# Attention on one core: shape blocks on TensorE in the step that forms scores, transposes and multiplies by v

## The chip, the cores and the metric

The kernel runs on one core of a Trainium2 chip. The metric is the device time of one execution in microseconds, the median of several runs.

## The reference, cut to what matters

Causal attention with a learned decay, for 4 batches of 8 heads with 576 positions and head size 64, in float32; then two feed-forward blocks on the 2304 tokens of 512 numbers.

```python
scores = scale * np.matmul(q, k.transpose(0, 1, 3, 2))
cum = np.cumsum(np.maximum(s, 0.0), axis=-1)
bias = -(cum[:, :, :, None] - cum[:, :, None, :])
scores = np.where(causal, -1000000000.0, scores + np.minimum(bias, 0.0))
scores = scores - np.max(scores, axis=-1, keepdims=True)
attn = np.exp(scores)
attn = attn / (np.sum(attn, axis=-1, keepdims=True) + 1e-09)
x = np.matmul(attn, v)                 # then heads side by side: (2304, 512)
a = x @ w1
b = x @ w2
x = (a * b @ w3) @ w_out               # first block
h = x @ w_in                           # second: softmax, a norm, and w_out
```

## The kernel before

**Work of a head.** The queries of a head are cut into five row tiles (the table QT): four of 128 rows, which see 576, 448, 320 and 192 keys, and one of 64 rows, which sees 64 keys. `qk_part(h, part)` forms the scores of tile 0 in a large PSUM buffer (part 0, two products of 288 columns), of tiles 1 and 4 in a small one (part 1), of tiles 2 and 3 in another (part 2), and `softmax_tile` (lines 205 and 209) takes the row maximum on VectorE and the exponential on ScalarE. Heads 0 to 7 form scores by one float32 product each (line 183), later heads by two of a faster type (lines 191 and 192), whose operands `split_qk` prepares. `normalise(h)` divides the rows by their sums (lines 236 to 244).

`tr_part(h, part)` transposes the weights of head h through TensorE into PSUM, and `evict` copies them into the tile PT of that head, on ScalarE and VectorE in turn (lines 92 and 94). Parts 0, 1 and 2 hold four, four and two transpositions of 128 by 128 (line 276). Three kinds of 64-by-64 blocks remain: the one of tile 4 (line 280, in part 2, on rows 0 to 63, issued behind the eviction of part 2's 256 columns from the same PSUM bank), and the four lower halves of the diagonal blocks (line 284, part 3, on rows 64 to 127). A head has fifteen transpositions and seven evictions.

`av_parts(p)` multiplies the transposed weights of a pair of heads with v. It makes twelve products of two heads each (line 308); each float32 product stands in the trace as two passes, so a pair has 24 records. The first is a product of 64 columns on 64 rows, then come 512, 448, 320 and 192 columns on 128 rows, and the last, for the keys 512 to 575, has 64 columns on 64 rows. The result is evicted from a large PSUM buffer into xT, as a coarse and a fine half. v is loaded by `load_v` into a tile `vr` with two buffers.

**Fillers.** `ab_unit` computes half a block of a and b, twelve products of 288 columns for each (line 336), for batches whose attention is done. Each of its two functions goes into the list `fill`.

**Order.** The loop from line 511 writes one step after the other. A step forms the scores of head h, transposes head ph = h - 2 and, behind every second one, has the products with v of that pair. NF says how many units a step adds to `fill`; F(1) to F(4) issue a quarter of the list each, at four places: between the parts of the scores, behind the first part of the transpositions, behind the third, and at the end. Pairs from head 10 on have their products with v put off: they become one entry, third in the next step's `fill`. At a step's end stand the loads for v and for the head after next (q, k and the rows of the cumulated sums, all on SyncE's queue) and `split_qk`.

This is the order of the program text. The framework's scheduler gives it to the engines by priority in that order, but moves an instruction ahead of others that it believes to be waiting, so the order on an engine can differ. From step 11 on, PSUM holds one large buffer (for scores of tile 0 and the products with v) and six small ones (for all else).

After attention the memory of its tiles is given back, and the stage loads of w3 and the first w_out begin (line 416), beside the a and b units of the last batch; then come the second block's products.

The few lines that set the order of a step:

```python
        if h is not None:
            qk_part(h, 1)
            F(1)
            qk_part(h, 2)
        if ph is not None:
            tr_part(ph, 0)
        F(2)
```

Of the kernel before, what the change touches and what calls it, by code (L numbers as in the profile page):

```python
# [8 lines left out]
F32 = mybir.dt.float32  # L9
# [16 lines left out]
def tile_attention_moe(  # L26
# [15 lines left out]
    nc = tc.nc  # L42
    B, H, D, _, S = qkT.shape
# [17 lines left out]
    QOF = {4: QT[0][3], 3: QT[1][3], 2: QT[2][3], 1: QT[3][3], 0: QT[4][3]}  # L61
# [13 lines left out]
    ident = const.tile([128, 128], F32, name="ident")  # L75
# [8 lines left out]
    def smalltile(name):  # L84
        return PSP[1].tile([128, 512], F32, tag="B", name=name)

    def flat(ap):
        return ap.rearrange("p a b -> p (a b)")

    def hi(dst, src, eng=None):  # L90
        if eng is None:
            nc.scalar.activation(out=dst, in_=src, func=AF.Copy)  # L92
        else:
            eng.tensor_copy(out=dst, in_=src)

    def lo(dst, src, hi_, eng=nc.vector):
        eng.tensor_tensor(out=dst, in0=src, in1=hi_.bitcast(F32), op=ALU.subtract)  # L97
# [3 lines left out]
    at = attn_ctx.enter_context(tc.tile_pool(name="at", bufs=1, side="left"))  # L101
# [12 lines left out]
    PT = [at.tile([128, KO[5]], F32, name=f"PT{i}") for i in range(4)]  # L114
# [1 line left out]

    after = [None]
    raw_t = {}
    v_t = {}
    VB = 2  # L120
    XHE = None

    def load_head(h):
# [12 lines left out]

    def load_v(p):
        b, hp = divmod(p, NP)
        vr = at.tile([128, 5, 2, D], F32, tag="vr", bufs=VB, name="vr")
        v_t[p] = vr  # L140
        nc.sync.dma_start(
            out=vr[:, 0:4].rearrange("p c e d -> p (c e d)"), in_=vM[b, hp],
        )
        nc.sync.dma_start(out=vr[0:64, 4].rearrange("p e d -> p (e d)"), in_=vE[b, hp])
# [10 lines left out]
    def ENG(h):  # L155
        if h < 8:
            return dict(QB=None, KA=None, QA=V, QL=G, KL=V)
        return dict(QB=None, KA=None, QA=V, QL=G, KL=G)
# [3 lines left out]
    def split_qk(h):  # L162
        if h < NQ:
            return
        q2, k2 = raw_t.pop(h)
        QA = at.tile([128, S], F32R, tag="QA", bufs=2, name="QA")
        KA = at.tile([128, S], F32R, tag="KA", bufs=2, name="KA")
        qb, kb = QB[h % 2], KB[h % 2]
        e = ENG(h)
        hi(qb[64:128], q2[64:128], e["QB"])  # L170
        hi(KA, k2, e["KA"])
        hi(QA[0:64], q2[0:64], e["QA"])
        lo(QA[64:128], q2[64:128], qb[64:128], e["QL"])
        lo(kb[64:128], k2[64:128], KA[64:128], e["KL"])
        qk_t[h] = (QA, KA)
# [70 lines left out]
    def half_view(t, j):  # L246
        a = t[0:64, KO[j]:KO[j] + 64]
        return bass.AP(a.tensor, a.offset, [list(a.ap[0]), [S - 128 * j, 2], [1, 64]])

    def tr_part(h, part):  # L250
        pt = p_t[h]
        PT_ = PT[h % 4]
        ps = smalltile("tr")

        def evict(dst, src):
            cnt[0] += 1
            hi(dst(PT_), src, PCOPY[cnt[0] % len(PCOPY)])

        def blk(j, q0, q1):
            o = KO[j] - 128 * j  # L260
            return lambda t: t[:, o + q0:o + q1]

        ev = []
        if part == 0:
            full = [(0, i, (i - 1) * 128) for i in range(1, 5)]
            ev = [(0, 512, blk(0, 64, S))]
        elif part == 1:
            full = [(1, i, (i - 2) * 128) for i in range(2, 5)] + [(3, 4, 384)]
            ev = [(0, 384, blk(1, 192, S)), (384, 512, blk(3, 448, S))]
        elif part == 2:  # L270
            full = [(2, i, (i - 3) * 128) for i in range(3, 5)]
            ev = [(0, 256, blk(2, 320, S))]
        else:
            full = []
        for j, i, c in full:
            nc.tensor.transpose(ps[:, c:c + 128], pt[:, QOF[i] + 128 * j:QOF[i] + 128 * j + 128], ident)  # L276
        for c0, c1, d in ev:
            evict(d, ps[:, c0:c1])
        if part == 2:
            nc.tensor.transpose(ps[0:64, 256:320], pt[0:64, QOF[0]:QOF[0] + 64], ident[0:64, 0:64])  # L280
            evict(lambda t: t[0:64, 0:64], ps[0:64, 256:320])
        if part == 3:
            for i in range(1, 5):
                nc.tensor.transpose(
                    ps[0:64, 64 * i:64 * i + 64],
                    pt[64:128, QOF[i] + 128 * i:QOF[i] + 128 * i + 64],
                    ident[64:128, 64:128],
                )
            for j in (1, 3):
                src = ps[0:64, 64 * j:64 * j + 128].rearrange("p (a b) -> p a b", a=2)  # L290
                evict(lambda t: half_view(t, j), src)
            p_t.pop(h)
# [3 lines left out]

    def av_parts(p):

        vr = v_t.pop(p)
        b, hp = divmod(p, NP)  # L300
        XH, XL = xT[b % 2]
        st = {}

        def mm(j, c0, c1, **kw):
            rows = 64 if j == 4 or c1 == 64 else 128
            o = KO[j] - 128 * j
            for e in range(2):
                nc.tensor.matmul(  # L308
                    st["ps"][64 * e:64 * e + 64, 448 + c0:448 + c1], vr[0:rows, j, e],
                    PT[(2 * p + e) % 4][0:rows, o + c0:o + c1], **kw,  # L310
                )

        def part(j):
            if j == 0:
                st["ps"] = flat(bigtile("av"))
                mm(0, 0, 64, start=True, stop=True)
            mm(j, 128 * j if j else 64, S, start=j == 0, stop=j == 4)
            if j == 4:
                ps = st["ps"]
                hi(XH[:, hp], ps[:, 448:1024], XHE)  # L320
                lo(XL[:, hp], ps[:, 448:1024], XH[:, hp])

        return [lambda j=j: part(j) for j in range(5)]
# [163 lines left out]
    for st in STAT:  # L487
        nc.gpsimd.memset(st, 1.0)
    for t in PT:
        for j in range(1, 4):  # L490
            nc.gpsimd.memset(t[64:128, KO[j]:KO[j] + 64], 0.0)
    split_qk(0)
    if NQ < 1:
        load_head(1)
# [9 lines left out]
    steps += [(None, H - 2), (None, H - 1)]  # L504
    steps += [(h if h < NH else None, h - 2 if h >= H + 2 else None) for h in range(H, NH + 2)]
    NF = {10: 3, 11: 0, 12: 3, 13: 0, 14: 3, 15: 2, 16: 2, 17: 0, 18: 1, 19: 1, 20: 1, 21: 2, 22: 2, 23: 2, 24: 2, 25: 2, 26: 2, 27: 2, 28: 2, 29: 2, 30: 2, 31: 2, 32: 2, 33: 2, 34: 3, 35: 3}
    PD, AVO = 10, 2
    PUMP = {3: 1, 5: 1, 6: 1, 10: 2, 11: 1, 12: 2, 13: 1, 14: 3, 15: 2, 16: 1, 17: 1}
    fill = []
    late = []  # L510
    for st, (h, ph) in enumerate(steps):
        for _ in range(NF.get(st, 0)):
            fill.extend(ab_unit(*units.pop(0)))
        if late:
            parts = late.pop()
            fill.insert(min(AVO, len(fill)), lambda parts=parts: [fn() for fn in parts])
        left = len(fill)
        if st == 11:
            ps_ctx.close()
            PSP[:] = [  # L520
                ps_ctx.enter_context(tc.tile_pool(name="psE", bufs=1, space=PSUM)),
                ps_ctx.enter_context(tc.tile_pool(name="psF", bufs=6, space=PSUM)),
            ]

        def F(k):
            while fill and len(fill) > left * (4 - k) // 4:
                fill.pop(0)()

        if h is not None:
            if NQ <= h + 2 < NH:  # L530
                load_head(h + 2)
            qk_part(h, 0)
        if st > 1:
            pump(PUMP.get(st, 0))
        if h is not None:
            qk_part(h, 1)
            F(1)
            qk_part(h, 2)
        if ph is not None:
            tr_part(ph, 0)  # L540
        F(2)
        if h is not None:
            normalise(h)
        if ph is not None:
            tr_part(ph, 1)
            tr_part(ph, 2)
            F(3)
            tr_part(ph, 3)
        if h is not None:
            if h % 2 == 1:  # L550
                load_v(h // 2)
            if h + 1 < NH:
                split_qk(h + 1)
            if h < 2 and h + 2 < NQ:
                aug_rows(QB[h], KB[h])
            if h + 2 < NH:
                if h + 2 < NQ:
                    load_head(h + 2)
                load_aug(h + 2, cumf_scr[h + 2:h + 3] if h + 2 < NQ else cum_scr[h + 2])
        F(4)  # L560
        if ph is not None and ph % 2:
            parts = av_parts(ph // 2)
            if ph < PD or st == len(steps) - 1:
                for fn in parts:
                    fn()
            else:
                late.append(parts)
# [180 lines left out]
    for i in range(8):  # L748
        c, o = divmod(i, 2)
# [48 lines left out]
    for t in range(NT + 2):  # L798
        c, o = divmod(t, 2)
# [68 lines left out]
```

## Time and profile before

| what | us |
|---|---|
| median of 3 runs (lowest, highest) | 797.59 (797.01, 799.87) |
| profiled execution | 799.96 |
| its span, first to last instruction | 798.1 |
| TensorE busy (products) | 767.1 (96%) |
| VectorE busy | 474.7 (59%) |
| ScalarE busy | 396.2 (50%) |
| GpSimd busy | 154.2 (19%) |
| mean granted clock of TensorE | 0.985 of full |

The profile is that of one execution. TensorE's products (PE) are pipelined: a product's record lasts longer than the time until the next one starts, and its end is modelled. So two times can be read: the length of a record, and the distance of two starts. PEld are the weight loads, which overlap the products. DVE is VectorE, ACT ScalarE, POOL GpSimd and SP SyncE; L336 is line 336 of the kernel. A form like 128\*64 is rows by columns of the loaded weights; 64x64 f32 behind it is what is written.

### The profile page before, as it was taken

What the parts mean: (1) busy time and instruction counts of PE and PEld (TensorE: products, weight loads), DVE (VectorE), ACT (ScalarE), POOL (GpSimd) and SP (SyncE); (2) the same over time, 40 slices, a digit from 0 to 9 for tenths busy, and PEclk for the clock granted to TensorE, in tenths of its full rate; (3) what the DMA queues carried; (4) which work ended last, traced back from release to release, by engine and by line L of the source; (5) the groups of instructions that cost most, each with busy time, mean ns of one, the idle gap of its engine ahead of it and who ended that gap; (6) DMA issues with size and microseconds to landing.
All of it is one profiled execution on the core that took longest, in us unless ns stands there. A gap on an engine that the chain in (4) does not pass through costs nothing.

```text
span 798.1 us, 13047 instructions
## 1 busy us (share of the span) xinstructions
PE 767.1 (96%) x4864; PEld 655.5 (82%) x4864; DVE 474.7 (59%) x1162; ACT 396.2 (50%) x927; POOL 154.2 (19%) x155
## 2 busy tenths in 40 slices
PE   7988899999999999999989979899999999999997
PEld 5555888878988888898988868788888888888886
DVE  5897699866565555325977999744344243533231
ACT  4986697896666566322435435533323233332232
POOL 6031323242122121002323345300000000000000
PEclk9998999999999999999999989899999999999999
DMA  5542465333332320105759555012020200000001
GB/s 145 180 138 81 120 193 175 87 119 92 105 90 77 105 61 31 46 30 177 239 167 315 187 184 185 15 53 67 14 67 23 70 14 14 14 14 14 14 27 39
DMA packets 38038, 75.58 MB, mean 95 GB/s; under 512 B 6796, under 2 KB 18060, under 8 KB 37976
## 3 DMA queue, kind: packets, MB, share of 16 engines
q1 hardware_dynamic: 37976, 74.76, 30.2%
q8 instruction: 38, 0.62, 0.3%
q14 instruction: 24, 0.20, 0.1%
HBM read 60.36 MB, written 14.38 MB: 94 GB/s over the span
## 4 chain that ended last, share of the span: by engine, by line
PE 77%; DVE 9%; DMA 6%; POOL 3%; issue 2%; ACT 1%; SPq 1%; POOLq 0%; ACTq 0%; DVEq 0%
PE o L737 13%; PE b L336 12%; PE a L336 11%; PE h L688 11%; PE x L668 10%; PE av L308 6%; PE tr L276 4%; DMA stage<-in_w_dram 3%; PE sc L191 2%; PE sc L192 2%; DVE stage L379 2%; PE tr L726 2%; PE sc L183 2%; DVE stage L378 2%; DVE stage L382 1%
## 5 line engine op out<-in xcount | busy, mean ns | idle before, releaser
L209 ACT ACTIVATE P<-P,STAT 64x64 f32<-64x64 f32 (+4 forms) x160 | 88.2, 554 | 53.1 <-DVE STAT L205 50.1
L696 DVE TENSOR_REDUCE sv<-h 128x1 f32<-128x1024 f32 x18 | 22.0, 1223 | 115.1 <-PE h L688 115.1
L668 PE MATMUL x<-gh,MH 128*128 128x256 f32 x288 | 83.7, 291 | 3.8 <-ACT MH L92 3.8
L205 DVE CUSTOM_DVE_ANT_0 P<-sc,wmask 64x64 f32<-64x64 f32 (+4 forms) x160 | 72.2, 481 | 22.9 <-PE sc L192 15.0
L668 PE MATMUL x<-gh,ML 128*128 128x256 f32 x288 | 81.9, 285 | 2.1 <-DVE ML L97 2.1
L668 PE MATMUL x<-gl,MH 128*128 128x256 f32 x288 | 82.1, 285 | 0.0
L97 POOL TENSOR_TENSOR QA<-qk,QB 64x576 fp32r<-64x576 f32 x24 | 37.7, 1569 | 218.3 <-ACT QB L92 179.3
L356 DVE TENSOR_TENSOR g_sb<-b,a_sb 128x288 f32<-128x288 f32 x64 | 28.9, 453 | 56.4 <-PE b L336 29.5
L710 POOL TENSOR_TENSOR sv<-sv,mhalf 128x1 f32<-128x1 f32 x18 | 10.0, 555 | 263.2 <-DVE sv L707 263.2
L336 PE MATMUL b<-xT1h,W 128*128 128x288 f32 x256 | 58.9, 302 | 1.5 <-ACT a_sb L348 1.5
L668 PEld LDWEIGHTS x<-gh,MH 128*128 128x128 f32 x288 | 56.0, 194 | 5.0 <-ACT MH L92 4.2
L336 PE MATMUL b<-xT0h,W 128*128 128x288 f32 x256 | 59.9, 305 | 0.0
L308 PE MATMUL av<-PT,vr 64*64 64x64 f32 (+4 forms) x384 | 58.8, 407 | 0.5 <-DVE STAT L205 0.3
L336 PE MATMUL a<-xT0h,W 128*128 128x288 f32 x256 | 58.7, 303 | 0.1
L688 PE MATMUL h<-IH,x2l 128*128 128x512 f32 x144 | 56.7, 394 | 1.7 <-DVE x2l L97 1.7
L336 PE MATMUL a<-xT1h,W 128*128 128x288 f32 x256 | 58.2, 301 | 0.0
L668 PEld LDWEIGHTS x<-gh,ML 128*128 128x128 f32 x288 | 55.9, 194 | 2.5 <-DVE ML L97 2.3
L737 PE MATMUL o<-OH,lh 128*128 128x512 f32 x144 | 57.2, 397 | 0.4 <-ACT lh L92 0.4
L737 PE MATMUL o<-OH,ll 128*128 128x512 f32 x144 | 57.1, 396 | 0.0
L737 PE MATMUL o<-OL,lh 128*128 128x512 f32 x144 | 56.9, 395 | 0.0
L668 PEld LDWEIGHTS x<-gl,MH 128*128 128x128 f32 x288 | 56.0, 194 | 0.8
L688 PE MATMUL h<-IL,x2h 128*128 128x512 f32 x144 | 56.5, 393 | 0.0
(124 smaller groups left out, 1984.1 us busy)
## 6 DMA issues: line engine op xcount, KB each, us to landing
stage<-in_w_dram SPq DMA_DIRECT2D x32, 512.0 KB
qk<-in_qk_dram SPq DMA_DIRECT2D x48, 288.0 KB
g_scr<-g_sb SPq DMA_DIRECT2D x32, 288.0 KB
stage<-in_wo_dram SPq DMA_DIRECT2D x16, 512.0 KB
graw<-g_scr SPq DMA_DIRECT2D x6, 1024.0 KB
out_dram<-o SPq DMA_DIRECT2D x18, 256.0 KB
vr<-in_vm_dram SPq DMA_DIRECT2D x16, 256.0 KB
stage<-in_w_in_dram SPq DMA_DIRECT2D x8, 512.0 KB
```

Of the source, the lines that this page charges most:

```text
L97: eng.tensor_tensor(out=dst, in0=src, in1=hi_.bitcast(F32), op=ALU.subtract)
L183: nc.tensor.matmul(view, QN[h % 2][:, q0:q0 + rows], KN[h % 2][:, c0:c0 + view.shape[-1]], start=True, stop=True,)
L205: nc.vector.tensor_tensor_reduce(out=dst2, in0=ps_in, in1=msk, scale=-SCALE, scalar=BIG, op0=ALU.add, op1=ALU.min, accum_out=st[0:rows, ti ...
L209: nc.scalar.activation(out=dst, in_=dst, func=AF.Exp, bias=st[0:rows, ti:ti + 1], scale=-1.0, accum_out=st[0:rows, 5 + ti:6 + ti],)
L276: nc.tensor.transpose(ps[:, c:c + 128], pt[:, QOF[i] + 128 * j:QOF[i] + 128 * j + 128], ident)
L308: nc.tensor.matmul(st["ps"][64 * e:64 * e + 64, 448 + c0:448 + c1], vr[0:rows, j, e], PT[(2 * p + e) % 4][0:rows, o + c0:o + c1], **kw,)
L336: nc.tensor.matmul(ps, w_[:, c, fs], x_[:, c, sl], start=(c == 0 and w_ is WH and x_ is XH), stop=(c == KC - 1 and w_ is WL),)
L356: nc.vector.tensor_tensor(out=g[:, sl], in0=ps, in1=st["a"], op=ALU.mult)
L668: nc.tensor.matmul(ps[m], w_[:, k, m * 128:m * 128 + 128], g_[:, k], start=(k == 0 and w_ is MH and g_ is GH), stop=(k == KF - 1 and w_ is ...
L688: nc.tensor.matmul(ps[:, hf], x_[:, k, ts_], w_[:, k, hf * 512:hf * 512 + 512], start=(k == 0 and x_ is XH and w_ is IH), stop=(k == KC - ...
L696: nc.vector.reduce_max(out=sv[:, 0:1], in_=psf, axis=AX.X, negate=True)
L737: nc.tensor.matmul(ps, l_[:, k], w_[:, k], start=(k == 0 and l_ is LH and w_ is OH), stop=(k == KF - 1 and l_ is LL),)
```

## The change

The v tiles become two fixed tiles VT, with zeros in rows 64 to 127 of the last block of keys; the transposed tiles PT get zeros in rows 64 to 127 of the first and the last diagonal block too (before, of the three between). With that the products of `av_parts` use 128 rows throughout. The transposition of line 280 is issued ahead of the evictions of its part. In a step the three parts of the scores follow each other (`pump` still stands behind the first), then half of the fillers, then `normalise`, the four parts of the transpositions, and the put-off products with v; the other half of the fillers comes at the end.

```diff
--- before.py
+++ after.py
@@ -116,8 +116,7 @@
 
     after = [None]
     raw_t = {}
-    v_t = {}
-    VB = 2
+    VT = [at.tile([128, 5, 2, D], F32, name=f"VT{i}") for i in range(2)]
     XHE = None
 
     def load_head(h):
@@ -136,8 +135,7 @@
 
     def load_v(p):
         b, hp = divmod(p, NP)
-        vr = at.tile([128, 5, 2, D], F32, tag="vr", bufs=VB, name="vr")
-        v_t[p] = vr
+        vr = VT[p % 2]
         nc.sync.dma_start(
             out=vr[:, 0:4].rearrange("p c e d -> p (c e d)"), in_=vM[b, hp],
         )
@@ -274,10 +272,11 @@
             full = []
         for j, i, c in full:
             nc.tensor.transpose(ps[:, c:c + 128], pt[:, QOF[i] + 128 * j:QOF[i] + 128 * j + 128], ident)
+        if part == 2:
+            nc.tensor.transpose(ps[0:64, 256:320], pt[0:64, QOF[0]:QOF[0] + 64], ident[0:64, 0:64])
         for c0, c1, d in ev:
             evict(d, ps[:, c0:c1])
         if part == 2:
-            nc.tensor.transpose(ps[0:64, 256:320], pt[0:64, QOF[0]:QOF[0] + 64], ident[0:64, 0:64])
             evict(lambda t: t[0:64, 0:64], ps[0:64, 256:320])
         if part == 3:
             for i in range(1, 5):
@@ -296,18 +295,17 @@
 
     def av_parts(p):
 
-        vr = v_t.pop(p)
+        vr = VT[p % 2]
         b, hp = divmod(p, NP)
         XH, XL = xT[b % 2]
         st = {}
 
         def mm(j, c0, c1, **kw):
-            rows = 64 if j == 4 or c1 == 64 else 128
             o = KO[j] - 128 * j
             for e in range(2):
                 nc.tensor.matmul(
-                    st["ps"][64 * e:64 * e + 64, 448 + c0:448 + c1], vr[0:rows, j, e],
-                    PT[(2 * p + e) % 4][0:rows, o + c0:o + c1], **kw,
+                    st["ps"][64 * e:64 * e + 64, 448 + c0:448 + c1], vr[:, j, e],
+                    PT[(2 * p + e) % 4][:, o + c0:o + c1], **kw,
                 )
 
         def part(j):
@@ -487,8 +485,10 @@
     for st in STAT:
         nc.gpsimd.memset(st, 1.0)
     for t in PT:
-        for j in range(1, 4):
+        for j in range(5):
             nc.gpsimd.memset(t[64:128, KO[j]:KO[j] + 64], 0.0)
+    for t in VT:
+        nc.gpsimd.memset(t[64:128, 4], 0.0)
     split_qk(0)
     if NQ < 1:
         load_head(1)
@@ -504,16 +504,13 @@
     steps += [(None, H - 2), (None, H - 1)]
     steps += [(h if h < NH else None, h - 2 if h >= H + 2 else None) for h in range(H, NH + 2)]
     NF = {10: 3, 11: 0, 12: 3, 13: 0, 14: 3, 15: 2, 16: 2, 17: 0, 18: 1, 19: 1, 20: 1, 21: 2, 22: 2, 23: 2, 24: 2, 25: 2, 26: 2, 27: 2, 28: 2, 29: 2, 30: 2, 31: 2, 32: 2, 33: 2, 34: 3, 35: 3}
-    PD, AVO = 10, 2
+    PD, FS = 10, 0.5
     PUMP = {3: 1, 5: 1, 6: 1, 10: 2, 11: 1, 12: 2, 13: 1, 14: 3, 15: 2, 16: 1, 17: 1}
     fill = []
     late = []
     for st, (h, ph) in enumerate(steps):
         for _ in range(NF.get(st, 0)):
             fill.extend(ab_unit(*units.pop(0)))
-        if late:
-            parts = late.pop()
-            fill.insert(min(AVO, len(fill)), lambda parts=parts: [fn() for fn in parts])
         left = len(fill)
         if st == 11:
             ps_ctx.close()
@@ -522,8 +519,8 @@
                 ps_ctx.enter_context(tc.tile_pool(name="psF", bufs=6, space=PSUM)),
             ]
 
-        def F(k):
-            while fill and len(fill) > left * (4 - k) // 4:
+        def F(share):
+            while fill and len(fill) > left * (1 - share):
                 fill.pop(0)()
 
         if h is not None:
@@ -534,18 +531,16 @@
             pump(PUMP.get(st, 0))
         if h is not None:
             qk_part(h, 1)
-            F(1)
             qk_part(h, 2)
-        if ph is not None:
-            tr_part(ph, 0)
-        F(2)
+        F(FS)
         if h is not None:
             normalise(h)
         if ph is not None:
-            tr_part(ph, 1)
-            tr_part(ph, 2)
-            F(3)
-            tr_part(ph, 3)
+            for part in range(4):
+                tr_part(ph, part)
+        if late:
+            for fn in late.pop():
+                fn()
         if h is not None:
             if h % 2 == 1:
                 load_v(h // 2)
@@ -557,7 +552,7 @@
                 if h + 2 < NQ:
                     load_head(h + 2)
                 load_aug(h + 2, cumf_scr[h + 2:h + 3] if h + 2 < NQ else cum_scr[h + 2])
-        F(4)
+        F(1)
         if ph is not None and ph % 2:
             parts = av_parts(ph // 2)
             if ph < PD or st == len(steps) - 1:
```

## Rows read from the trace of the kernel before

**Rows 1.** Busy time by stretch (the first line names the columns), four stretches of the span.

```profile
core 0: us, PE busy (x) PEld busy (x) DVE busy (x) ACT busy (x) POOL busy (x), PEclk, DMA share, GB/s
40.00:60.00 20.00, 17.32 (x92) 10.17 (x92) 19.77 (x62) 17.94 (x49) 6.43 (x3) 1.00 0.46 139
60.00:80.00 20.00, 17.63 (x105) 11.43 (x105) 15.64 (x43) 13.11 (x34) 2.43 (x2) 0.83 0.27 78
100.00:364.00 264.00, 262.71 (x1947) 225.96 (x1946) 159.64 (x506) 168.20 (x452) 58.36 (x40) 1.00 0.32 92
290.80:295.20 4.40, 4.40 (x36) 2.53 (x34) 3.73 (x11) 3.65 (x9) 3.10 (x2) 1.00 0.01 2
```

**Rows 2.** Who TensorE waited for, from 100 to 364 us.

```profile
engine line waited for: us in total, times, longest us
PE tr L284 <- DVE STAT L205: 0.9, 1, 0.9
PE av L308 <- DVE STAT L205: 0.3, 1, 0.3
```

**Rows 3.** Timeline of SyncE's queue around the end of attention.

```profile
start us, us, engine line op out<-in xcount [idle before <-releaser]
...
364.08 1.76 SPq L416 DMA_DIRECT2D stage<-in_wo_dram  x4
```

**Rows 4.** Timeline of TensorE from 283.6 to 287 us.

```profile
283.55 0.29 PE L336 MATMUL a<-xT0h,W 128*128 128x288 f32 x1
283.77 0.41 PE L284 MATMUL tr<-ident,P 64*64 64x64 f32 x4
284.11 0.40 PE L336 MATMUL b<-xT0h,W 128*128 128x288 f32 x1
284.35 0.29 PE L336 MATMUL b<-xT0l,W 128*128 128x288 f32 x1
284.48 0.43 PE L336 MATMUL b<-xT0h,W 128*128 128x288 f32 x2
284.75 0.29 PE L336 MATMUL b<-xT0l,W 128*128 128x288 f32 x1
284.88 0.30 PE L336 MATMUL b<-xT0h,W 128*128 128x288 f32 x1
285.11 0.24 PE L280 MATMUL tr<-ident,P 64*64 64x64 f32 x1
285.28 0.40 PE L336 MATMUL b<-xT0h,W 128*128 128x288 f32 x1
285.51 0.29 PE L336 MATMUL b<-xT0l,W 128*128 128x288 f32 x1
...
286.59 0.19 PE L191 MATMUL sc<-KB,QB 128*64 128x64 f32 x1
286.62 0.22 PE L192 MATMUL sc<-KA,QA 128*64 128x64 f32 x1
286.68 0.38 PE L336 MATMUL a<-xT0h,W 128*128 128x288 f32 x1
286.89 0.30 PE L336 MATMUL a<-xT0l,W 128*128 128x288 f32 x1
```

**Rows 5.** Timeline of TensorE from 288.2 to 295.5 us.

```profile
288.43 0.33 PE L308 MATMUL av<-PT,vr 64*64 64x64 f32 x2
...
291.40 3.21 PE L308 MATMUL av<-PT,vr 64*64 64x64 f32 x22
```

**Rows 6.** Groups by line from 100 to 364 us: count | busy us, mean ns | idle before.

```profile
L284 PE MATMUL tr<-ident,P 64*64 64x64 f32 x96 | 9.9, 223 | 0.9 <-DVE STAT L205 0.9
...
L94 DVE COPY PT<-tr 64x128 f32<-64x128 f32 (+5 forms) x84 | 31.1, 383 | 15.5 <-ACT PT L92 7.6 <-PE tr L276 2.9 <-PE tr L284 2.4
...
L92 ACT ACTIVATE PT<-tr 64x128 f32<-64x128 f32 (+5 forms) x84 | 27.2, 348 | 6.6 <-PE tr L276 2.9 <-DVE PT L94 2.3 <-PE tr L280 1.0
```

**Rows 7.** Groups by line of GpSimd, first 30 us.

```profile
L491 POOL MEMSET PT<- 64x64 f32 x12 | 1.2, 148 | 0.2
```

## The prediction

> **What bounds the kernel now.** I read the table by stretch first, then who waited on TensorE, then the timeline. In the stretch from 100 to 364 us, which holds the attention of 24 of the 32 heads, TensorE is busy 262.71 of 264.00 us at granted clock 1.00, while VectorE has 159.64, ScalarE 168.20 and GpSimd 58.36 us of work [rows 1]. TensorE waited there for others twice, 0.9 and 0.3 us, and never for a DMA [rows 2]. So the order and the pace of TensorE's own instructions set the end of this stretch, and a microsecond taken out of its queue is a microsecond of the span. Before 100 us this holds less: from 40 to 60 us TensorE is busy 17.32 of 20 us and VectorE 19.77 [rows 1]. After 364 us the four stage loads of the next phase are issued at 364.08 us [rows 3], right behind the last product with v; they use memory that attention gives back, so what follows moves with attention's end.
>
> "Busy" hides the loss that matters here; the starts show it. In a row of products of one shape (128 rows by 128 columns, 288 columns moving) four products from 284.35 to 284.88 us take 0.53 us, 0.133 each. When one 64-by-64 transposition (line 280) stands among them, from the product at 284.88 to the second product after it, at 285.51, are 0.63 us. Two products in that span account for 0.265. With four transpositions of line 284 the same span, 283.55 to 284.35, is 0.80 us: three more cost 0.17, 0.057 each. So one visit to the 64-row shape costs 0.63 - 0.265 - 0.057 = 0.31 us beyond its work, 0.155 for each change of shape, going in and coming out [rows 4]. During that time TensorE counts as busy, because a product's record is simply longer (0.40 in place of 0.29 us).
>
> The order on the engine isn't the program's, since the scheduler moves work past what it believes to be waiting. In a pair of heads in mid-stretch I count in the timeline: the four transpositions of line 284 apart, twice (once per head); line 280's apart, twice, since its bank is being evicted when the program issues it; the first 64-row half of the product with v apart at 288.43, three microseconds ahead of the rest at 291.40 [rows 5]; and the rest, which goes from full tiles into 64-row products, into 128-row products, back to 64 rows and out. That is 2 x 2 + 2 x 2 + 2 + 4 = 14 changes per pair, besides one visit of the scores' last tile per head. The stretch has 96 transpositions of line 284 [rows 6], four to a head: 24 heads, 12 pairs.
>
> **The change, part by part.** *Line 280 ahead of the evictions, and the four parts of the transpositions in one block.* The 64-row transpositions of a head (one of line 280, four of line 284) come next to each other: one visit per head, where there were two. Work is unchanged: as many transpositions, evictions and bytes.
>
> *128 rows throughout in the products with v.* The two 64-column products become 128-row ones. Columns, instructions and weight columns are as many as before, so I cost the products themselves at nothing. The two changes inside the block go, and with the products in one shape behind the transpositions the visit before it is left into them: full tiles, 64-row transpositions, 128-row products with v, full tiles: three changes. A pair of heads then has 2 + 3 = 5 changes in place of 14. Nine fewer x 0.155 x 12 pairs = **16.7 us**. What this trace doesn't show cleanly is the change between a product with v (128 rows, 64 columns) and a full tile: the nearest rows are the scores' last tile, of the same shape: its visit, 286.59 to 286.89 us, takes 0.30 us, of which the full product behind it has 0.133 and two 64-column products 0.03 each (286.59 to 286.62), so that 0.11 is left for both changes, where a 64-row visit has 0.31 [rows 4]; that would make the way out cheaper by up to 0.155, 12 x 0.155 = 1.9 us more gain; the far bound is the 0.31 of a whole visit, 1.9 us less. I take 0.155, the price of the visits in whose company it stands.
>
> The Trainium skill (TensorEngine Tiling (Array Packing), Key Properties) says that a change of tiling mode, not of the tile alone, drains the engine, and lists 128x64 as a mode of its own. By that rule the way out of the products with v is a full change, as taken; by the scores' rows it is cheaper and the sum 1.9 us lower. The trace agrees with the rule for 64-row tiles and shows less than it says for the scores' last tile.
>
> *What is left over.* The scheduler will still move instructions. I leave one visit too many in every third head: 8 x 0.31 = 2.5 us lost (bounds: none, and one in every head, 24 x 0.31 = 7.4).
>
> *The first eight heads.* Four pairs, 9 changes less each: 4 x 9 x 0.155 = 5.6 us at most; VectorE is nearly full there [rows 1], so nothing is the other bound. I take half, 2.8.
>
> *Fillers in two places and not four.* The same 24-product units are issued. Their old role, to cover waits for softmax, is kept by the half that stands between the scores and the transpositions, and by the scheduler. I cost it at nothing as long as TensorE waits for nobody [rows 2]; if the cover is gone, the price is the second rival's.
>
> *Normalisation of the new head now stands ahead of the first transposition's eviction on VectorE and ScalarE, and the products with v ahead of the end-of-step loads and splits.* The transpositions belong to a head two steps older, whose tile is ready. In their way is only an eviction that starts later; TensorE has six small PSUM buffers. The v load into one of two buffers still waits for the products with v of two pairs back, one step earlier, and behind it on the DMA queue stand the bias rows and the next q and k loads, which TensorE doesn't wait for in this stretch [rows 2]. The first products of the next step's scores need the large PSUM buffer that the products with v use; the second half of the fillers (24 products, 3.2 us, where a step has two units) covers its eviction. Nothing, twice.
>
> *Ten more memsets on GpSimd at the start* (eight on the transposed tiles, two on the v tiles), beside twelve that take 148 ns each [rows 7]: 1.5 us if all stand ahead of the bias rows that start the scores, 0 if none. The scheduler places them where GpSimd would wait, so I take 0.5, nearer to none.
>
> **Sum.** -16.7 + 2.5 - 2.8 + 0.5 = -16.5 us. The profiled execution took 799.96 us (span 798.1 and 1.9 around it), so the changed kernel would take 783.5 in it. It lies 2.4 us above the median of the runs, 797.59, so in the terms of the median the forecast is **781.0 us**.
>
> **Rivals.** *The blocks don't stay blocks.* The scheduler pulled even one product's two halves apart [rows 5]; if it pulls fillers into the blocks wherever it believes a tile late, only what no order can undo is left, the two changes inside the products with v: 12 x 2 x 0.155 = 3.7 us, and the time is 793.9. Against it: line 280's place ahead of the evictions takes away what made it late.
>
> *The transpositions wait for their evictions.* A head has (84 + 84)/24 = 7 evictions, 383 ns on VectorE and 348 on ScalarE [rows 6], now asked for in one burst while both engines also have the new head's softmax. If each head's block stands still for one eviction of either engine, 0.73 us, 24 of them are 17.5 us and eat the gain: 798.6. Against it: both engines have a third of the stretch free [rows 1] and the scheduler would put a filler there, a visit for 0.31 and not a wait for 0.73.
>
> *The clock falls (slower).* From 60 to 80 us, where the first steps have no fillers and TensorE worked mostly on transpositions and products with v with waits between, the granted clock was 0.83, a part of it at the lower level, 1.2 GHz; 17% of 20 us is 3.4 us [rows 1]. If the block of transpositions and products with v, now without a filler in it, brings such a fall in each of 12 pairs, 41 us come on top: 822. It decides from five falls on (16.5/3.4). Against it: from 290.80 to 295.20 us the trace already has ten transpositions and 22 products with v in a row, 4.40 us of TensorE, at clock 1.00 [rows 1], and the new block is no longer.
>
> The Trainium skill (TensorE: Matmul & The Clock Gate, Part 4: PE-mode transpose) says that transpositions don't count as busy for the clock as products do; by it a denser block of them would speak for this rival. That the stretch around 291 us kept its clock speaks against it.
>
> **How the numbers follow.** Forecast 0.84; blocks undone 0.06; eviction waits 0.05; clock 0.05. The forecast's own range: all of its best bounds together, -16.7 - 1.9 - 5.6 = -24.2, give 773; the worst, -16.7 + 1.9 + 7.4 + 1.5 = -5.9, give 792. No more than 2 in 10 lies outside 773 to 792, so this is the range. A measurement can tell 0.5%, 4 us, from no change. The forecast counts as faster, with a hundredth from the first rival's better half: faster 0.85; the first two rivals are the rest of same, 0.10; the clock is slower, 0.05.
>
> **What would show it.** Right: in the timeline between two filler groups one block of ten full and five 64-row transpositions, in every second step followed by 24 products with v all of form 128*64; visits to 64 rows about one per head; the stretch of the last 24 heads near 250 us; still no waits of TensorE there; the first stage load of the next phase 15 to 18 us earlier and everything after it shifted alike. Wrong: as many lone visits of lines 280 and 284 as now (first rival); TensorE waiting for PT evictions in the waits (second); granted clock under 1.00 between 100 and 350 us (third); or an attention that ends earlier while the span keeps its length, which would refute that the later phase hangs on its end.

## The result, and the profile after

The changed kernel takes 788.55 us (median of 4 runs, 786.89 to 790.51) against 798.61 us on the same chip, ratio 0.9864, 95% interval 0.9827 to 0.9902: 10.1 us faster, by over 0.5% and inside the forecast range, but 7.5 us over the 781.0 foretold. Of the 16.5 us forecast 10.1 came. Its profiled execution has a span of 788.7 us, against 798.1.

The busy time by stretch of the changed kernel (columns as in [rows 1]):

```profile
core 0: us, PE busy (x) PEld busy (x) DVE busy (x) ACT busy (x) POOL busy (x), PEclk, DMA share, GB/s
40.00:60.00 20.00, 15.93 (x91) 9.96 (x91) 18.07 (x57) 16.81 (x47) 5.84 (x4) 1.00 0.40 113
60.00:80.00 20.00, 18.51 (x113) 13.26 (x114) 16.79 (x46) 13.67 (x36) 4.35 (x3) 0.83 0.40 116
100.00:165.00 65.00, 61.77 (x448) 54.80 (x447) 54.30 (x157) 49.72 (x129) 19.23 (x12) 0.95 0.46 133
165.00:352.00 187.00, 187.00 (x1471) 169.02 (x1471) 103.91 (x344) 116.22 (x314) 37.91 (x26) 1.00 0.28 80
```

From 165 us to the end of attention TensorE is never idle and has its full clock. From 100 to 165 us, where the weights w1 and w2 are converted beside attention, it is idle for 3 us, its clock falls to 0.95, and VectorE is busy 54 of 65 us. The stretch of [rows 1] from 100 us on is two stretches with different limits.

Who TensorE waited for, from 100 to 165 us; from 165 to 352 us the same view names nobody:

```profile
engine line waited for: us in total, times, longest us
PE a L334 <- ACT a_sb L346: 1.8, 1, 1.8
PE a L334 <- ACT PT L92: 0.7, 1, 0.7
PE tr L283 <- DVE STAT L203: 0.5, 1, 0.5
PE b L334 <- DVE g_sb L354: 0.2, 1, 0.2
```

The timeline of TensorE in two neighbouring steps (lines 274, 276, 283, 306 and 334 of the changed kernel are 276, 280, 284, 308 and 336 of the old one):

```profile
274.69 0.30 PE L334 MATMUL b<-xT0h,W 128*128 128x288 f32 x1
274.83 1.25 PE L274 MATMUL tr<-ident,P 128*128 128x128 f32 x10
276.01 0.24 PE L276 MATMUL tr<-ident,P 64*64 64x64 f32 x1
276.01 0.41 PE L283 MATMUL tr<-ident,P 64*64 64x64 f32 x4
276.36 0.40 PE L189 MATMUL sc<-KB,QB 128*128 128x288 f32 x1
...
284.44 1.26 PE L274 MATMUL tr<-ident,P 128*128 128x128 f32 x10
285.63 0.24 PE L276 MATMUL tr<-ident,P 64*64 64x64 f32 x1
285.63 0.41 PE L283 MATMUL tr<-ident,P 64*64 64x64 f32 x4
285.97 2.93 PE L306 MATMUL av<-PT,VT 128*64 128x64 f32 x24
```

Here is the block as the program writes it: ten full transpositions, the five small ones together, and in the second step all 24 records of the products with v behind them, in one shape. Where [rows 4, 5] show three visits and a split product, one visit per head is left. SyncE issues the next phase's stage loads at 352.41 us, 11.7 us earlier than in [rows 3] (15 to 18 were forecast):

```profile
352.41 0.81 SPq L414 DMA_DIRECT2D stage<-in_wo_dram  x2
```

### The profile page after: what moved, and what is told of

Same layout as the page of the kernel before. It is cut to its first block, busy times and chain, and to the rows that moved or that the text cites. A ratio compares the mean times of both kernels' runs of the same rounds, so it can differ in the third digit from the quotient of the medians.

```text
span 788.7 us, 13075 instructions
## 1 busy us (share of the span) xinstructions
PE 756.8 (96%) x4864; PEld 658.4 (83%) x4864; DVE 472.9 (60%) x1162; ACT 396.5 (50%) x927; POOL 157.7 (20%) x165
## 4 chain that ended last, share of the span: by engine, by line
PE 75%; DVE 6%; DMA 3%; POOL 2%; issue 2%; ACT 2%; SPq 0%; ACTq 0%; DVEq 0%; POOLq 0%
PE o L732 13%; PE a L334 12%; PE b L334 11%; PE h L683 11%; PE x L663 11%; PE av L306 4%; PE tr L274 3%; PE sc L189 3%; PE sc L190 2%; PE m L589 2%; PE tr L721 2%; DMA stage<-in_w_dram 2%; DVE stage L377 1%; DVE stage L376 1%; DVE stage L380 1%
## 5 line engine op out<-in xcount | busy, mean ns | idle before, releaser
L207 ACT ACTIVATE P<-P,STAT 128x448 f32<-128x448 f32 (+4 forms) x160 | 87.9, 551 | 30.0 <-DVE STAT L203 28.6
L97 POOL TENSOR_TENSOR QA<-qk,QB 64x576 fp32r<-64x576 f32 x24 | 34.6, 1441 | 208.9 <-ACT QB L92 170.1
L203 DVE CUSTOM_DVE_ANT_0 P<-sc,wmask 128x448 f32<-128x448 f32 (+4 forms) x160 | 70.2, 478 | 9.5 <-PE sc L181 6.5
L334 PE MATMUL b<-xT1h,W 128*128 128x288 f32 x256 | 57.0, 297 | 2.9 <-DVE g_sb L354 2.8
L334 PE MATMUL b<-xT0h,W 128*128 128x288 f32 x256 | 58.2, 302 | 0.2 <-DVE g_sb L354 0.2
L683 PE MATMUL h<-IH,x2h 128*128 128x512 f32 x144 | 56.2, 390 | 0.0
L693 ACT ACTIVATE e<-h,sv 128x1024 f32<-128x1024 f32 x18 | 20.1, 1115 | 66.7 <-DVE sv L691 66.7
```

Source lines behind the costliest of these rows:

```text
L203: nc.vector.tensor_tensor_reduce(out=dst2, in0=ps_in, in1=msk, scale=-SCALE, scalar=BIG, op0=ALU.add, op1=ALU.min, accum_out=st[0:rows, ti ...
L207: nc.scalar.activation(out=dst, in_=dst, func=AF.Exp, bias=st[0:rows, ti:ti + 1], scale=-1.0, accum_out=st[0:rows, 5 + ti:6 + ti],)
L334: nc.tensor.matmul(ps, w_[:, c, fs], x_[:, c, sl], start=(c == 0 and w_ is WH and x_ is XH), stop=(c == KC - 1 and w_ is WL),)
L683: nc.tensor.matmul(ps[:, hf], x_[:, k, ts_], w_[:, k, hf * 512:hf * 512 + 512], start=(k == 0 and x_ is XH and w_ is IH), stop=(k == KC - ...
L693: nc.scalar.activation(out=e, in_=psf, func=AF.Exp, bias=sv[:, 0:1], scale=1.0, accum_out=sv[:, 1:2])
```

## The experiments

Two numbers are read from each trace besides the time. The *stretch* runs from the last product with v of pair 7 (about 180 us) to the end of attention: the last eight pairs. In it I counted the *changes* between full tiles, 64-row tiles and products with v; the scores' last tile, which every kernel has alike, is not counted. "Outside" is the change of the median against the kernel before on the same chip, less the change of the stretch.

| kernel | median, before beside it | ratio (95%) | stretch us | changes | outside us |
|---|---|---|---|---|---|
| before (two profiles) | - | - | 183.38, 183.38 | 105 | - |
| order alone | 802.39, 798.48 | 1.0048 (1.0029, 1.0067) | 179.62 | 83 | +7.7 |
| line 280 alone | 803.93, 798.48 | 1.0072 (1.0043, 1.0101) | 181.17 | 95 | +7.7 |
| 128 rows alone | 795.02, 798.48 | 0.9956 (0.9939, 0.9972) | 181.08 | 90 | -1.2 |
| order and line 280 | 793.39, 798.81 | 0.9932 (0.9906, 0.9957) | 172.94 | 51 | +5.0 |
| all three (the change) | 788.55, 798.61 | 0.9864 (0.9827, 0.9902) | 170.49 | 43 | +2.8 |
| the change, again | 788.75, 798.08 | 0.9877 (0.9840, 0.9914) | 170.47 | 43 | +3.6 |
| old order to step 17 | 786.88, 798.48 | 0.9852 (0.9830, 0.9874) | 170.47 | 43 | +1.3 |
| the same, again | 784.29, 798.08 | 0.9824 (0.9796, 0.9852) | 170.47 | 43 | -0.9 |
| first steps as before | 787.93, 798.81 | 0.9882 (0.9830, 0.9933) | 170.47 | 43 | +2.0 |

**What one change of shape costs.** Three kernels put one more instruction, which nothing reads, ahead of each group of twelve products of a and b in the changed kernel:

```diff
             for c in range(KC):
+                if c == 0:
+                    nc.tensor.transpose(pw[0:64, 448:512], ident[0:64, 0:64], ident[0:64, 0:64])
```

> The changed kernel with one more 64-by-64 transposition of the identity ahead of each of the 128 groups of twelve products of a and b (nothing reads it). Theory: each is a visit to the 64-row shape, 0.31 us beyond 0.057 of work, start to start; 128 x 0.37 = 47 us, about 836. Rival (a 64-by-64 transposition costs its work, and what was seen was waiting): 128 x 0.06 to 0.11, 796 to 803.

```diff
+                    nc.tensor.matmul(pw[0:64, 448:512], ident[:, 0:64], ident[:, 0:64], start=True, stop=True)
```

> As the run before, with a float32 product of 128 rows and 64 columns of the identity, 64 columns moving (the shape of a product with v), in place of the transposition. If this shape is a full change against full tiles: 2 x 0.053 of work and 0.31, 0.42 each, 53 us in all, 842. If it is as cheap as the scores' last tile: 0.107 and 0.11, 0.22 each, 28 us, 816.

```diff
+                    nc.tensor.transpose(pw[:, 384:512], ident, ident)
```

> The changed kernel with one more 128-by-128 transposition ahead of each of the 128 groups of twelve products: twice the rows and columns of the 64-by-64 one, but no change of shape. Theory of changes: 0.109 each and nothing besides, 14 us in all where every one counts, at most 802, against 823 with the quarter-size ones. Rival (any foreign instruction between products costs 0.3): 823 or more.

Their times, one run each, are 823.06, 827.09 and 794.25 us; the second lies between its two expectations, so the starts have to decide. One such place in the timeline of each, first the 64-by-64 one:

```profile
283.53 0.29 PE L337 MATMUL a<-xT1h,W 128*128 128x288 f32 x1
283.76 0.24 PE L335 MATMUL b<-ident 64*64 64x64 f32 x1
283.93 0.40 PE L337 MATMUL b<-xT1h,W 128*128 128x288 f32 x1
284.17 0.30 PE L337 MATMUL b<-xT1l,W 128*128 128x288 f32 x1
```

then that of 128 rows and 64 columns:

```profile
284.82 0.29 PE L337 MATMUL a<-xT1h,W 128*128 128x288 f32 x1
285.04 0.33 PE L335 MATMUL b<-ident 128*64 128x64 f32 x2
285.30 0.40 PE L337 MATMUL b<-xT1h,W 128*128 128x288 f32 x1
285.54 0.30 PE L337 MATMUL b<-xT1l,W 128*128 128x288 f32 x1
```

and the full one:

```profile
328.77 0.30 PE L337 MATMUL a<-xT0h,W 128*128 128x288 f32 x1
328.91 0.27 PE L335 MATMUL b<-ident 128*128 128x128 f32 x1
328.93 0.38 PE L337 MATMUL b<-xT0h,W 128*128 128x288 f32 x1
329.15 0.29 PE L337 MATMUL b<-xT0l,W 128*128 128x288 f32 x1
```

Read from the first start to the last, these are 0.64, 0.72 and 0.38 us, of which the two products have 0.265. The full transposition, four times the size, costs 0.115, just its work (ten in a row take 1.18 us in the timeline above, 274.83 to 276.01); the quarter-size one costs 0.375, and the product of 64 columns 0.455. In the stretch, which holds 64 of the 128 groups, the kernels take 192.82, 198.03 and 177.73 us: 22.3, 27.6 and 7.3 us more than the changed kernel, or 0.35, 0.43 and 0.11 per group (up to 0.03 of each is other work, two to ten more products of a and b). So not any foreign instruction costs 0.3 us, but the change of shape does, and the shape of the products with v is at least as dear a change as 64 rows (0.43 - 0.107 of work is 0.32; in the place shown 0.72 - 0.265 - 0.107 = 0.35). Over the whole kernel the extra is less than 128 times that (34.5 us, not 47). Outside the stretch TensorE is idle 3 to 5 us less than in the two profiles of the changed kernel, so that a part is hidden in waits; the rest of the difference is not accounted for.

One rival is left by these three kernels: a product with v is float32 and its neighbours are of the faster type, so the change of type could be what costs. The trace of the kernel before has the case apart. In the first heads the scores are float32 throughout, and the last tile, of 128 rows and 64 columns, stands between full tiles of the same type:

```profile
L183 PE MATMUL sc<-KN,QN x8: 222/420/540, 8.7 to 10.7; 128*128 128x288 f32 x2, 128*128 128x448 f32 x2, 128*64 128x64 f32 x2, 128*128 128x320 f32 x2
```

In the single records the last 448-column pass starts at 9.55 us, the two passes of the small tile at 10.02 and 10.13, and the two 320-column passes at 10.28 and 10.65. From 9.55 to 10.65 are 1.10 us. Where the next pass is of the same shape, one of 448 columns takes 0.377 and one of 320 takes 0.268, and the two small ones have 0.107 of work, so 0.35 is left for the visit. The type did not change, so the price is that of the shape.

**The parts of the change, alone and in pairs.** Only the order of the step (the diff's last hunks):

> The kernel before with only the new order of a step: scores in one block, fillers in two places, the four parts of the transpositions in a block, products with v behind them; line 280 still behind its evictions and 64-row products with v. Theory (every change between the 64-row and the 128-row shape costs 0.155 us on TensorE): counted in the program's own order, changes fall only from 216 to 200, 122 to 104 of them for heads 14 to 31, because line 280 is still late and is moved away; 16 x 0.155 = 2.5 us less, about 796. Rival (the blocks themselves bring it: fewer interruptions by fillers): most of the 10 us, about 789.

Only line 280:

```diff
+        if part == 2:
+            nc.tensor.transpose(ps[0:64, 256:320], pt[0:64, QOF[0]:QOF[0] + 64], ident[0:64, 0:64])
         for c0, c1, d in ev:
             evict(d, ps[:, c0:c1])
         if part == 2:
-            nc.tensor.transpose(ps[0:64, 256:320], pt[0:64, QOF[0]:QOF[0] + 64], ident[0:64, 0:64])
```

> The kernel before with only line 280's transposition issued ahead of the evictions of its part. Theory of changes: 216 to 205 in the program's order, 11 x 0.155 = 1.7 us less, about 797; no difference that can be told. Rival (the late transposition held up the evictions and the products with v behind it): 4 us or more less, 794 or under.

Only the 128-row products with v:

```diff
-            rows = 64 if j == 4 or c1 == 64 else 128
...
-                    st["ps"][64 * e:64 * e + 64, 448 + c0:448 + c1], vr[0:rows, j, e],
-                    PT[(2 * p + e) % 4][0:rows, o + c0:o + c1], **kw,
+                    st["ps"][64 * e:64 * e + 64, 448 + c0:448 + c1], vr[:, j, e],
+                    PT[(2 * p + e) % 4][:, o + c0:o + c1], **kw,
```

> The kernel before with only the 128-row products with v (fixed v tiles, ten more memsets). Theory of changes: 216 to 191, 25 x 0.155 = 3.9 us less, about 795. Rival (going from 128-row, 64-column products to full tiles is as dear as from 64 rows, so only the two changes inside a block count, and the memsets cost up to 1.5 us): 16 pairs x 2 x 0.155 - 1.5 = 3.5 us less at most and perhaps 2.

The changed kernel with the old `mm` of `av_parts` (that last edit undone):

> The changed kernel with the old 64-row products with v. Theory: 216 to 146 changes in the program's order, 122 to 63 for heads 14 to 31, 59 x 0.155 = 9.1 us gained from 165 us on; with the loss of steps 10 to 17 some 6 us under the kernel before, about 792. Order alone gained 18 changes there and line 280 alone 10, so that together they must bring more than their sum (28): line 280 ready in time is what lets the block stay a block. Rival (the three parts add up, 128 rows bring the most): slower than before by 5 us or more, as order alone and line 280 alone were.

The stretch gets shorter with the count of changes in every one of them, by 0.15 to 0.22 us for each. 128 rows alone take 15 changes and 2.3 us away; order alone 22 changes and 3.8 us, line 280 alone 10 and 2.2; the two together 54 changes and 10.4 us, far more than the 32 and 6.0 of their sum. Either alone leaves the small transpositions apart, in 31 groups over the stretch, where the kernel before has 30; with both they stand in 16, and the block stays a block. So much is as the theory has it, and so are the times of 128 rows alone (795.02, about 795 expected) and of order and line 280 (793.39, about 792). But order alone and line 280 alone are *slower* kernels, by 3.9 and 5.5 us, where 2.5 and 1.7 us less were expected: outside the stretch each loses 7.7 us. That neither theory had.

The two views of line 280 alone that show where, busy time from 100 to 165 us and who TensorE waited for there:

```profile
100.00:165.00 65.00, 59.25 (x415) 50.29 (x414) 57.61 (x159) 49.18 (x123) 19.68 (x12) 0.97 0.45 136
```

```profile
PE av L309 <- DVE STAT L205: 2.4, 1, 2.4
PE b L337 <- DVE STAT L205: 1.0, 1, 1.0
PE sc L191 <- DVE g_sb L357: 0.9, 2, 0.5
PE a L337 <- DVE PT L94: 0.6, 1, 0.6
PE sc L191 <- DVE STAT L205: 0.5, 1, 0.5
PE sc L191 <- issue: 0.3, 1, 0.3
```

and the same stretch in the second profile of the kernel before:

```profile
100.00:165.00 65.00, 63.70 (x474) 54.66 (x473) 57.49 (x166) 53.57 (x140) 20.73 (x14) 1.00 0.50 146
```

VectorE has the same 57.5 us of work in both; TensorE gets through 474 products in the one and 415 in the other. Moving one small transposition per head made the scheduler order these steps otherwise, and TensorE is idle 5.7 us, nearly all of it waiting for VectorE, where it had been idle 1.3; its clock is 0.97. The waits are a part of the loss only. From the end of pair 3 to the end of pair 7 line 280 alone takes 107.1 us, of which TensorE is idle 5.8; the two profiles of the kernel before take 99.3 and 103.2 and are idle 3.6 and 4.5.

**Can the first steps be kept out of it?** The changed kernel with the old order in steps 0 to 17:

```diff
+            if st < NEW:        # NEW = 18
+                F(1)
             qk_part(h, 2)
+        if ph is not None and st < NEW:
+            tr_part(ph, 0)
...
+            if st < NEW:
+                tr_part(ph, 1)
+                tr_part(ph, 2)
+                F(3)
+                tr_part(ph, 3)
+            else:
+                for part in range(4):
+                    tr_part(ph, part)
```

> The changed kernel with the old order of a step (fillers in four places, first transpositions ahead of normalise) in steps 0 to 17 and the new one from step 18. Theory (in steps 10 to 16, where weights are converted beside attention, the blocks leave TensorE waiting for ScalarE and VectorE and bring a lower clock, 5 to 6 us lost): no waits of TensorE and clock 1.00 from 100 to 140 us, unit 14 of a and b no later than before, and the span 4 to 6 us under the changed kernel, about 784. Rival (that stretch is bound by VectorE's and ScalarE's conversions whatever the order): the same time as the changed kernel within 2 us, 787 to 790.

And with line 280's old place too, for heads below 14 (`if part == 2 and h >= 14` at the new place, `h < 14` at the old):

> 128-row products with v throughout, the old order of a step and the old place of line 280 for steps 0 to 17 (heads below 14), the new order and place after. Theory (two stretches: from step 18 on TensorE alone sets the pace and 0.155 us per change of shape is gained; in steps 10 to 17, where weights are converted beside attention, any other order of the old kernel costs waits): about as 128 rows alone to 165 us (1 to 2 us ahead of the kernel before), then 12 to 13 us gained to the end of attention, in all about 14, a time of 783 to 785, less than the changed kernel's. Rival (the loss in steps 10 to 17 comes by itself with whatever is nearby, or the later phase takes back all that goes beyond 10 us): 787 to 789, as the changed kernel.

Both have the stretch of the changed kernel to 0.02 us. The first came out 1.7 us under the changed kernel's first median, which is its rival's case (within 2 us), and with waits left (its clock from 120 to 145 us is 0.93), which speaks against its theory. The second has 0.9882 of the time of the kernel before, the changed kernel 0.9864, so it is not under it at all. Three kernels were run again, to see how far one program moves:

> The changed kernel once more, for a second profile. If the loss in steps 10 to 17 belongs to its order, TensorE again waits there for ScalarE and VectorE, and the lead over the kernel before again shrinks by 4 to 5 us between the ends of pair 3 and pair 7 (81 and 180 us before); if it was chance of one execution, the lead at pair 7 stays near that of pair 3. The stretch from pair 7 to the end of attention again 170.5 us. Time 787 to 790.

> The kernel with the old order of a step to step 17, again, beside the changed kernel on the same chip. Theory that the old order saves something in steps 10 to 17: 1 to 2 us under the changed kernel. Rival (what costs there is line 280's new place, which both have): no difference.

> The kernel before once more, for a second profile: how far its own ends of pair 3 and pair 7 move between two executions. If by under 1 us, the differences of 3 to 7 us in steps 10 to 17 are of the orders; if by 3 us or more, they cannot be told from chance. The stretch from pair 7 to the end of attention again 183.4 us.

Against the first profile of the kernel before, its second one is 2.7 us ahead at the end of pair 3 and 1.2 us behind at the end of pair 7: by what the expectation says, differences of 3 us between those two places in single profiles can't be told from chance. What moved is mostly the clock. In the second profile TensorE waits 3.17 us for VectorE, as its timeline has it,

```profile
90.26 0.74 PE L191 MATMUL sc<-KB,QB 128*128 128x448 f32 x1 [3.17 <-DVE g_sb L356]
```

and then works at the lower level of its clock, 1.2 GHz (busy time from 90 to 95 us, the clock is the 0.50):

```profile
90.00:95.00 5.00, 4.74 (x19) 4.35 (x20) 5.00 (x15) 3.23 (x7) 1.77 (x2) 0.50 0.01 2
```

In the first profile the same wait is 2.27 us and the clock stays at 1.00. From the end of pair 3 to that of pair 7 the mean granted clock is 1.00 in the first and 0.97 in the second, 3.4 of the 3.9 us between them; idle time is 0.9.

What does repeat is the waiting. From 100 to 165 us TensorE is idle 1.3 us in both profiles of the kernel before, and 3.2 and 3.7 us in those of the changed one. The changed kernel's two profiles are 3.6 and 5.5 us ahead at pair 3 and 1.2 us behind and 1.5 ahead at pair 7. The 7.7 us of order alone and line 280 alone rest on medians with intervals, and on 6.8 and 9.4 us of lag at pair 7, well outside the two profiles of the kernel before (0 and 1.2).

Beside each other on one chip, the old order to step 17 took 784.29 us and the changed kernel 788.75; the intervals of their ratios, 0.9796 to 0.9852 and 0.9840 to 0.9914, overlap a little. Its 8 runs in all are 783.4 to 787.7 us, the changed kernel's 10 are 782.8 to 791.9. It is the fastest kernel measured here; that it beats the changed one is likely (by 1.7 and 4.5 us against the two medians) and not settled.

## Why the prediction was right or wrong

**The price of a change of shape (0.155 us): right, a little low.** The added visits measured it apart from all else: 0.32 us a visit in the place shown, 0.29 on average over the stretch. In the stretch 62 changes fewer go with 12.9 us; some 1.9 us of that is work which the changed kernel does outside it (5 small transpositions and 4 score products ahead of it, 8 products of a and b behind it), so 11.0 us are left, 0.177 each. Half of the 0.35 us of a visit to the float32 shape of the products with v is 0.175.

**The way out of the products with v: the value taken was right.** The scores' rows, which made it cheaper, misled: with float32 products this shape is a full change, 0.32 to 0.35 us a visit. The Trainium skill (TensorEngine Tiling (Array Packing), Key Properties, with the list under Available Configurations) says that changing the tiling mode drains the engine, and has 128x64 as a mode. The price measured for float32 products fits that; for the scores' last tile, of the faster type, the 0.11 us of [rows 4] stand against it.

**Nine changes fewer in a pair: nearly right in the last eight pairs.** Over the last eight pairs 62 changes went, 7.75 a pair; the kernel before had 13.1 a pair and not quite 14. Of the eight visits left over by the forecast none is there: 16 visits to 64 rows for 16 heads. For these eight pairs the forecast's terms give 8 x 9 x 0.155 = 11.2, less two thirds of 2.5, 9.5 us, against 12.9.

**"12 pairs", the step that failed.** I took the stretch from 100 us as one because TensorE was busy 262.71 of 264.00 us in it, and the count of one pair in its middle as that of all. Counted in the traces as in the table, the changes go only from 48 to 32 over pairs 4 to 7, four a pair and not nine, and from 51 to 39 over the first four pairs. So 28 changes went for the first 16 heads, 4.3 us at 0.155, where nine a pair would be 72 (the forecast took the first four pairs by half).

The waits took a part of even that. From 100 to 165 us VectorE is nearly as full as TensorE, 57.5 of 65 us in the second profile of the kernel before; there the old order happened to leave TensorE only 1.3 us of waits, and that was a property of this one order, not a reserve. For the first 16 heads the forecast has the rest, 16.5 - 9.5 = 7.0 us. The two profiles of each kernel give a lead of 0.7 us at the end of pair 7, on average, or 1.5 us with the transpositions and scores that are ahead. Up to there TensorE is idle 15.1 and 13.5 us in the changed kernel, 13.7 and 13.4 in the kernel before, so that idle time takes 0.7 us; what took the other 2 us of the 4.3 is not known. At the end of pair 3 the mean lead is 3.2 us, about what was forecast for the first eight heads (2.8 less 0.5), though the changed kernel has 14 products of a and b less behind it there, 1.9 us of work; the 4.7 us of pairs 4 to 7 did not come.

That the total lies in the range is partly luck: the last eight pairs brought 3.4 us more than the forecast's terms, the first 16 heads 6.3 us less, and 2.4 us were lost behind attention.

**Everything behind attention shifts alike: nearly.** Attention ends 13.6 us earlier in the mean of two profiles each (16.5 forecast) and the spans are 11.2 us apart; the last batch and the conversions of the next weights gave 2.4 us back. Of these 1.1 are the eight products of a and b put off to behind attention's end (383 records there, where the kernel before has 375). In the first profile of the changed kernel the lead falls from 11.7 us to 7.5 between 352 and 409 us, where TensorE waits 2.8 us for VectorE to multiply a by b, and is 9.4 at the end. The medians show 10.1 and 9.3.

**The parts are independent: never said, but the sum took it so.** Order and line 280 are worth 10.4 us in the stretch together and 6.0 apart. Order alone shows the first rival's mechanism, blocks that don't stay blocks. Without the 128 rows, the 3.7 us that the rival keeps, it would have no gain and no loss by that rival, and it lost 3.9 us, so the rival's 793.9 was too low a guess.

**The other rivals and terms.** From 165 to 352 us TensorE waits for no eviction, so the second rival is refuted there; from 100 to 165 us one such wait shows in the first profile (0.7 us, for an eviction of line 92). The clock is 1.00 from 165 to 352 us, through all blocks of 15 transpositions and 24 products with v in a row. By the Trainium skill (TensorE: Matmul & The Clock Gate, Part 4: PE-mode transpose) transpositions don't count as busy for the clock as products do. In these blocks, where the 15 take 1.5 us between products, that cost nothing. The sign of the third rival did show before: the clock is 0.95 from 100 to 165 us, which is 3.3 us at full clock, and there it is lowest where TensorE had waited 1.8 us for ScalarE:

```profile
130.00:140.00 10.00, 7.88 (x47) 6.67 (x45) 9.96 (x28) 8.93 (x25) 3.62 (x2) 0.83 0.62 170
```

The memsets' 0.5 us is not seen: the first score product starts at 8.14 us, in the kernel before at 8.13.

What stays open: why order alone and line 280 alone lose 7.7 us outside the stretch. Their waits are seen, but they are a part only, and which choice of the scheduler makes the loss was not isolated.

## What to carry to other kernels

Where TensorE is busy all the time, look at the distance of starts: an instruction of another tile shape between full ones costs 0.31 to 0.35 us beyond its work here (0.11 for the scores' last tile, of the faster type), and busy time hides it. Count the changes in the order that the engines really get, for a part of an edit may bring nothing alone: the small transpositions came together only when both their order and their readiness were changed. And split a stretch by what else runs in it, and count in each part, before multiplying by its length; in a part where a second engine is nearly as full, an order that leaves few waits is easily lost.

## What the runs showed that I had not expected

- The last eight pairs take the same time to 0.02 us in five profiles of three kernels that issue them almost alike (170.47 and 170.49), while the end of pair 7 moves by 5.5 us among them (177.9 to 183.4 us). Between the two profiles of the kernel before, the difference up to there is idle time and the granted clock: a wait of 3.17 us in place of 2.27 was followed by 1.2 GHz in one of them.
- The shape of 128 rows and 64 columns is a full change with float32 products (0.32 to 0.35 us a visit, next to float32 full tiles too) and nearly free with the faster type of the scores (0.11).
- A transposition one quarter the size costs three times as much as a full one (0.375 and 0.115 us).
